# Step 0's q first on GpSimd's queue, another order of the attention steps, routing one step earlier

## The chip, the cores and the metric

One core of a Trainium2 chip runs the whole kernel. The metric is the device time of one execution in microseconds; the time before is the median of three runs.

## The reference

Attention with normalised q and k over 8 batches, 12 heads, 448 tokens and 64 columns a head, then a layer of 8 experts to which each token is routed by a hash of its id.

```python
def _attn_ref(q, k, v, g_q, g_k):          # (8, 12, 448, 64)
    q_n, k_n = rmsnorm(q, g_q), rmsnorm(k, g_k)      # x / sqrt(mean(x*x) + 1e-6) * g
    scores = scale * np.matmul(q_n, k_n.transpose(0, 1, 3, 2))
    attn = np.exp(scores - max); attn = attn / (sum + 1e-9)
    return np.matmul(attn, v)
def _moe_ref(x, token_ids, w1, w2):        # x (3584, 768), w1 (8, 768, 1024), w2 (8, 1024, 768)
    expert_idx = token_ids * 2654435761 % 8
    for e in range(8):
        out[mask] = np.maximum(x[mask] @ w1[e], 0) @ w2[e]
```

## The kernel before

The kernel has an attention stage and an expert stage. In both the order on each engine is the order of the code (`manual_schedule`).

**Attention** runs in 48 steps (`NS`), six a batch; step s holds a pair of heads. What a step needs is made by short operations that the code names with two-letter words. `sqq`, `sqk` square q and k (`prep_sq`, L359, on VectorE, or on ScalarE with the flag `@A`); `sumq`, `sumk` add the squares up by 16 matmuls with the identity (`prep_sum`, L379); `redq`, `redk` reduce them (L394, VectorE); `ln` and `er` give the reciprocal root on ScalarE (L401, L405); `nq`, `nk` multiply by it (L415, VectorE); `Tq`, `Tk` transpose on PE (L576); `qT`, `kT` copy the transposes to SBUF (L598, VectorE, or ScalarE with `@A`). `sc:s.j` is one of the four score products of step s (L620), `exp:s.j` its exponential on ScalarE (L637: 896 columns, or 448 for j = 3), `av:s.p` the product with v (L647), `rec` and `x` the division on VectorE (L679, L686). `v:c` copies a chunk of v (L436). `zero:n` clears parts of buffers (L732), `gain:n` prepares the gains of k (L188), `spin:n` issues n matmuls of 448 columns on a cleared tile, whose result nobody reads (L779).

The order is written out by hand as a text of such words: one for the first two batches, with step and group numbers, and one named `steady`, which runs once for each of the other six. `emit` (L842) turns it into instructions.

PSUM holds three double banks for scores (`ps_sc`), one bank for sums and transposes (`ps_qk`) and one for the product with v. Sums and transposes with the flag `@S` take one of the score banks instead (`turn_bank`, L374). Steps 0 and 5 stand alone; the others are prepared in pairs. Step 0's and 5's q and k transposes lie in one and the same bank.

Step 0's q and k come in fp32 through the queues of SyncE and ScalarE (`load_heads`, `load_one_q`); the other q, k and v through GpSimd's queue, pair by pair, then batch by batch, in the order of the code. A load on GpSimd's queue waits, among others, for the load eight places ahead of it. `hooks` (L792) puts loads of later batches, of weights, and the **routing** into certain steps: `SIDE` and `AV_SIDE` (L784 to L790) name for each step the routing's VectorE operations (m1 to m15) and its small matmuls (m5a, m7a, m13a, m14a), which write into the bank of that step's product with v. From the routing come row numbers (`gidx`), by which GpSimd gathers the first three tiles of expert 0's tokens; `early_xT` (L632) transposes them in score banks.

**Experts**: eight times two products, 480 or 512 token columns wide: `gemm1` (L941) with a ReLU on ScalarE or VectorE, then `gemm2` (L956) in four token tiles, copied from PSUM by ScalarE and VectorE in turn and scattered to the output by GpSimd (L975). The last tile of all (`last`) has 96 tokens and goes out in two copies, 512 columns and 256, and one scatter. Weights come through GpSimd's queue; expert 2's lie in the first buffers of q and k.

## Time and profile before

| | before |
|---|---|
| median of three timed runs | 345.65 us (344.89 to 346.58) |
| the profiled execution | 343.94 us |
| its span, first to last instruction | 342.4 us |
| PE, matmuls | 327.5 us (96%) |
| PE, weight loads | 228.6 us (67%) |
| VectorE | 201.8 us (59%) |
| ScalarE | 188.6 us (55%) |
| GpSimd | 147.7 us (43%) |

In the page's 40 slices ScalarE and VectorE read 8 or 9 tenths through the first half, the attention, and 1 to 4 in the second, the experts; PE reads 9 from the second slice to the last but one. The shares of the whole span are means over two stages with different limits, so the stages are read apart. Times in all rows are microseconds from the span's start, unless marked ns.

### The profile page before, as it was taken

Reading aid. Unit: us, or ns where it says so; the run is one execution under the profiler, and the core shown is the slowest. Engines: PE = TensorE matmul, PEld = TensorE weight load, DVE = VectorE, ACT = ScalarE, POOL = GpSimd, SP = SyncE. Lnnn points to the kernel's source line nnn. Section 1 sums busy time; section 2 is a strip of 40 time slices with the busy share of each in tenths; the row PEclk is TensorE's granted clock in tenths of the full one; section 3 lists DMA queues with packets and bytes.
Section 4 is the critical chain, followed back from the end, with each engine's and each line's share of the span. In section 5 each row is a group of like instructions: output and inputs, shape, how many; then the busy total and the mean of one; then the engine's idle time right before and its main releaser. Section 6 shows DMA issues by size and latency. Waiting matters only on the chain. (4 is left out here: it accounts for less than half of the span.)

```text
span 342.4 us, 9198 instructions
## 1 busy us (share of the span) xinstructions
PE 327.5 (96%) x3893; PEld 228.6 (67%) x3893; DVE 201.8 (59%) x433; ACT 188.6 (55%) x286; POOL 147.7 (43%) x203
## 2 busy tenths in 40 slices
PE   4999999999999999999999999999999999999992
PEld 2577777776777777666677767677676776767761
DVE  3799999998989899976693243232332323323210
ACT  3599999999999999989442212212122120220210
POOL 8799935225330100003555854538555474202122
PEclk9999999999999999999999999999999999999997
DMA  8999999999999999032579899999999999403012
GB/s 138 217 200 202 202 236 200 239 202 227 201 244 211 254 210 233 13 82 71 127 147 247 169 204 249 261 278 244 252 272 262 259 243 278 174 0 133 22 79 88
DMA packets 42498, 64.80 MB, mean 189 GB/s; under 512 B 9687, under 2 KB 30623, under 8 KB 42200
## 3 DMA queue, kind: packets, MB, share of 16 engines
q0 software_dynamic: 38688, 58.09, 84.1%
q1 hardware_dynamic: 3456, 5.90, 5.6%
q8 instruction: 31, 0.51, 0.6%
q10 hardware_dynamic: 312, 0.21, 0.2%
q14 instruction: 11, 0.09, 0.1%
HBM read 89.29 MB, written 17.30 MB: 311 GB/s over the span
## 5 line engine op out<-in xcount | busy, mean ns | idle before, releaser
L642 ACT ACTIVATE expT<-sc_ps 128x896 bf16<-128x896 f32 x144 | 125.5, 973 | 1.6 <-PE sc_ps L626 1.3
L962 PEld LDWEIGHTS <-h_sb 128*128 128x128 f16 (+1 forms) x512 | 51.2, 104 | 30.0
L962 PE MATMUL o_ps<-w_sb,h_sb 128*128 128x512 f16 (+3 forms) x384 | 66.2, 326 | 0.0
L975 POOL DMA_INDIRECT out_dram<-o_sb,gidx x32 | 33.9, 1058 | 65.2 <-ACT o_sb L972 31.3
L949 ACT ACTIVATE h_sb<-h_ps 128x480 f16<-128x480 f32 (+1 forms) x36 | 19.9, 552 | 68.1 <-PE h_ps L945 68.1
L229 POOL DMA_INDIRECT kr<-x_scratch,gidx x32 | 33.5, 1047 | 52.1 <-DVE gidx L557 37.8
L945 PEld LDWEIGHTS <-w_sb 128*128 128x128 f16 x288 | 38.9, 136 | 16.2
L945 PE MATMUL h_ps<-xT,w_sb 128*128 128x480 f16 x240 | 49.4, 366 | 0.0
L972 ACT COPY o_sb<-o_ps 128x768 f32<-128x768 f32 x16 | 12.8, 798 | 61.4 <-PE o_ps L962 61.4
L951 DVE TENSOR_SCALAR h_sb<-h_ps 128x480 f16<-128x480 f32 x28 | 18.4, 658 | 47.2 <-PE h_ps L945 47.2
L626 PE MATMUL sc_ps<-qT,kT 64*128 64x448 f16 x288 | 44.5, 356 | 1.4 <-ACT expT L642 0.7
L660 PEld LDWEIGHTS <-expT 128*128 128x128 bf16 x864 | 37.8, 97 | 10.1 <-DVE x_sb L691 4.4
L660 PE MATMUL av_ps<-v,expT 128*128 128x65 bf16 x864 | 43.3, 193 | 0.1
L972 DVE COPY o_sb<-o_ps 128x768 f32<-128x768 f32 (+1 forms) x15 | 14.3, 956 | 31.5 <-PE o_ps L962 27.2
L691 DVE TENSOR_TENSOR x_sb<-av_ps,srec 128x448 f16<-128x448 f32 x48 | 29.9, 622 | 1.4
L303 POOL DMA_DIRECT2D vr<-in_v_dram x36 | 23.8, 671 | 15.6 <-DMA kr<-in_k_dram 6.8
L645 ACT ACTIVATE expT<-sc_ps 128x448 bf16<-128x448 f32 x48 | 29.4, 613 | 0.0
L384 PEld LDWEIGHTS <-ident 128*128 128x128 f16 x576 | 23.0, 99 | 8.5 <-issue 4.8
L241 DVE COPY xT<-xT_ps 128x768 f16<-128x768 f16 x25 | 13.8, 552 | 22.6 <-PE xT_ps L240 22.4
L665 PE MATMUL av_ps<-v,expT 128*128 128x130 bf16 x144 | 25.0, 220 | 0.0
L962 PE MATMUL o_ps<-kr,h_sb 128*128 128x512 f16 (+3 forms) x128 | 22.1, 326 | 0.0
L626 PEld LDWEIGHTS <-kT 64*128 64x128 f16 x288 | 12.6, 93 | 11.4 <-issue 2.5
(211 smaller groups left out, 453.0 us busy)
## 6 DMA issues: line engine op xcount, KB each, us to landing
w_sb<-in_moe_w_dram POOLq DMA_DIRECT2D x18, 512.0 KB, 10.9
w_sb<-in_moe_w_dram POOLq DMA_DIRECT2D x8, 768.0 KB, 13.7
kr<-in_k_dram POOLq DMA_DIRECT2D x7, 672.0 KB, 14.3
qr<-in_q_dram POOLq DMA_DIRECT2D x7, 672.0 KB, 12.5
x_scratch<-x_sb SPq DMA_DIRECT2D x15, 288.0 KB, 6.1
w_sb<-in_moe_w_dram POOLq DMA_DIRECT2D x2, 1536.0 KB, 26.5
qr<-in_moe_w_dram POOLq DMA_DIRECT2D x6, 512.0 KB, 15.6
vr<-in_v_dram POOLq DMA_DIRECT2D x14, 192.0 KB, 11.7
```

Of the source, the lines that this page charges most:

```text
L229: nc.gpsimd.indirect_dma_start(out=xg[0:idx.shape[0], :], out_offset=None, in_=x_dram[0:rows, :], in_offset=bass.IndirectOffsetOnAxis(ap=i ...
L303: eng.dma_start(out=dst[64 * half:64 * half + 64, :, s0:s0 + cnt, :].rearrange("p n s d -> p n (s d)"), in_=runs(t, h0 + HP * hh, 1, n, to ...
L626: nc.tensor.matmul(sc[:, hh, :S], lhsT=kT[64 * hh:64 * hh + 64, P * j:P * j + P], rhs=qT[64 * hh:64 * hh + 64, :], start=True, stop=True)
L642: nc.scalar.activation(expT[:, 2 * j:2 * j + 2, :], sc[:, :, :S], AF.Exp, bias=0.0, scale=1.0)
L645: nc.scalar.activation(expT[:, 6, :], sc[:, 0, :S], AF.Exp, bias=0.0, scale=1.0)
L660: nc.tensor.matmul(av[:, 2 * t + hh, :], lhsT=expT[:, tl(hh, j), P * t:P * t + P], rhs=v8[:, i, vs(hh, j), 0:D + 1], start=(hh == 0 and t ...
L665: nc.tensor.matmul(av[:, 2 * t:2 * t + 2, :], lhsT=expT[:, 6, P * t:P * t + P], rhs=v8[:, i, 0::7, 0:D + 1], start=False, stop=False)
L691: nc.vector.tensor_tensor(out=xs[b][:, :, hp * D:hp * D + D], in0=av[:, :, :D], in1=srec[:, :, None].to_broadcast([P, SL, D]), op=ALU.mult)
L945: nc.tensor.matmul(h_ps[:, :c1 - c0], lhsT=w1v[:, co, fo, :], rhs=xT[:, co, c0:c1], start=(co == 0), stop=(co == CO - 1))
L962: nc.tensor.matmul(o_ps[d0 > 0][0:w, d0:d1], lhsT=h_sb[:, fo, col * P:col * P + w], rhs=w2_sb[:, fo, d0:d1], start=(fo == 0), stop=(fo == ...
L972: (nc.vector.tensor_copy if col % 2 else nc.scalar.copy)(o_sb[0:w], o_ps[0][0:w])
L975: scat = nc.gpsimd.indirect_dma_start(out=out[:, :], out_offset=bass.IndirectOffsetOnAxis(ap=idx[0:w], axis=0), in_=o_sb[0:w], in_offset=N ...
```

## The change

- Step 0's two q loads go first on GpSimd's queue, ahead of all other loads there; before, one was on SyncE's and one on ScalarE's. The loads of the gains move from ScalarE's queue to SyncE's, and that of the token ids behind the loads of step 5.
- The text of the order is another one. In the first two batches: all clears of VectorE stand in front; 17 warming matmuls, then 2, 4 and 5, stand where 6, 5, 4 and 3 were; step 0's sums and transposes use score banks; the squares of step 1's k and of step 5's k go to ScalarE, k's copies of steps 0, 5 and 8 to VectorE, q's copy of step 0 to ScalarE; steps 3 and 4, and 6 and 7, are interleaved otherwise. In the steady text some words change places.
- A step that stands alone has a bank for each of its two transposes.
- `SIDE`, `AV_SIDE` and the early gathers come one step earlier.
- The 256 columns of the last tile are copied by ScalarE instead of VectorE.
- Expert 2's second weight comes in two loads of half the size.

```diff
--- before.py
+++ after.py
@@ -124,7 +124,7 @@
 
     def setup():
         for c, src in enumerate((g_q, g_k)):
-            nc.scalar.dma_start(out=grow[:, c],
+            nc.sync.dma_start(out=grow[:, c],
                                 in_=bass.AP(tensor=src.tensor, offset=src.offset,
                                             ap=[[0, 1], [0, 2], [1, D]]))
     def setup1():
@@ -211,7 +211,9 @@
     def load_w2(e, w2_sb, dyn=None):
         src = moe_w2[e] if dyn is None else moe_w2[bass.ds(dyn, 1)].rearrange("o f d -> (o f) d")
         rows = "(fo p) d -> p fo d" if e == 0 else "(p fo) d -> p fo d"
-        nc.gpsimd.dma_start(out=w2_sb[:], in_=src.rearrange(rows, fo=FO))
+        n = FO // 2 if e == 2 else FO
+        for f in range(0, FO, n):
+            nc.gpsimd.dma_start(out=w2_sb[:, f:f + n], in_=src.rearrange(rows, fo=FO)[:, f:f + n])
         return w2_sb
 
     def new_w1(pool):
@@ -582,9 +584,7 @@
                     nc.tensor.transpose(T[:, P * o:P * o + P],
                                         n8[:, x].rearrange("p i d -> p (i d)"), ident16[:])
                 return
-            if (s, 1) not in qkt:
-                qkt[s, 1] = qkt[s, 0] = ps_qk.tile([P, 512], FP32, name="qkT_ps")[:].bitcast(FP16)
-            T = qkt[s, a]
+            T = qkt[s, a] = turn_bank(flag).bitcast(FP16)
             n8 = n8_one[:, 4 * a:4 * a + 4 + a].rearrange("p x i d -> p x (i d)")
             if not a:
                 for x in range(4):
@@ -746,6 +746,7 @@
                 nc.scalar.copy(raw(1, HP - 1)[:, 0::7], z[:, 0:2])
                 nc.scalar.copy(raw(0, HP - 1)[64:P, 3::4], z[64:P, 0:2])
                 load_one(HP - 1)
+                setup1()
             elif part == 6:
                 zero_kv(V, v_bufs[0])
             elif part == 7:
@@ -754,9 +755,8 @@
                 V.memset(v8_all[0:64, :, :, 7, D], 0.0)
 
         load_heads([nc.sync, nc.scalar, nc.sync, nc.scalar], first[:, 1:2], k, 0, 1)
-        load_one_q([nc.sync, nc.scalar], first[:, 0], 0)
+        load_one_q([nc.gpsimd] * 2, first[:, 0], 0)
         setup()
-        setup1()
         nc.vector.memset(warm, 0.0)
         load_pairs(k, k_bufs, 0, 1, 0, HP, 2)
         make_identity(nc, ident16[:])
@@ -781,13 +781,13 @@
                 nc.tensor.matmul(wps[:, 0:448], lhsT=warm[:, 0:P], rhs=warm[:, 0:448],
                                  start=True, stop=True)
 
-        AV_SIDE = {NS - 11: (m5a, m5b), NS - 10: (m7a, m7b), NS - 5: (m14a, m14b)}
+        AV_SIDE = {NS - 12: (m5a, m5b), NS - 11: (m7a, m7b), NS - 6: (m14a, m14b)}
         for i in range(2):
-            AV_SIDE[NS - 7 + i] = (lambda av, i=i: m13a(av, i), lambda av, i=i: m13b(av, i))
+            AV_SIDE[NS - 8 + i] = (lambda av, i=i: m13a(av, i), lambda av, i=i: m13b(av, i))
         half = lambda f, *es: [lambda e=e: f(e) for e in es]
-        SIDE = {NS - 12: (m1, m2, m3), NS - 11: (m4,), NS - 9: [m8, m9] + half(m10, 0, 1),
-                NS - 8: half(m11, 0, 1) + half(m12, 0), NS - 7: half(m12, 1), NS - 6: (n2,),
-                NS - 4: (m15,), NS - 3: (n3,)}
+        SIDE = {NS - 13: (m1, m2, m3), NS - 12: (m4,), NS - 10: [m8, m9] + half(m10, 0, 1),
+                NS - 9: half(m11, 0, 1) + half(m12, 0), NS - 8: half(m12, 1), NS - 7: (n2,),
+                NS - 5: (m15,), NS - 4: (n3,)}
 
         def hooks(s):
             if s >= NS:
@@ -801,8 +801,8 @@
                 load(4, "kv")
             if hp == 3 and 1 <= b and b + 4 < B:
                 load(b + 4, "qkv")
-            if NS - 4 <= s < NS - 5 + KT:
-                c = s - NS + 4
+            if NS - 5 <= s < NS - 6 + KT:
+                c = s - NS + 5
                 gather(xg_e[:, c], gidx[:, c:c + 1], N_EARLY)
             if s == 24:
                 w_tiles[0] = [load_w1(0, new_w1(w_pool))]
@@ -858,46 +858,46 @@
         emit("""
-            zero:0 zero:2 zero:7 zero:3 spin:6 sqk:0.0 sqq@A:0.0 sumk:0.0 zero:6 redk:0.0
-            sqk:1.0 sumq:0.0 ln:0.1.2 spin:5 sumk@S:1.0 zero:1 er:0.1.2 nk:0 redq:0.0
...
+            zero:0 zero:1 zero:2 zero:6 zero:7 spin:17 sqk:0.0 zero:3 sqq@A:0.0 sumk@S:0.0
+            redk:0.0 sumq@S:0.0 ln:0.1.2 redq:0.0 er:0.1.2 ln:0.0.1 er:0.0.1 sqk@A:1.0
...
         steady = """
-            sc:0.3 exp:0.1 exp:0.3 av:-1.0 av:-1.1 av:-1.2 nq:2 sc:1.0 kT:2 rec:-1 x:-1
-            exp:1.0 Tq:2 qT:2 sc:1.1 sc:1.2 av:0.0 sc:1.3 av:0.1 sumk:1.0 exp:1.1 nk:4
...
+            exp:0.3 av:-1.0 av:-1.1 nq:2 av:-1.2 kT:2 sc:1.0 exp:1.0 rec:-1 x:-1 Tq:2 sc:1.1
+            sc:1.2 exp:1.1 qT:2 av:0.0 sqq:2.0 sc:1.3 exp:1.2 sumk:1.0 nk:4 av:0.1 exp:1.3
...
@@ -971,7 +971,7 @@
                 o_sb = m_o.tile([P, DIN], FP32, name="o_sb")
                 (nc.vector.tensor_copy if col % 2 else nc.scalar.copy)(o_sb[0:w], o_ps[0][0:w])
             else:
-                nc.vector.tensor_copy(o_sb[0:w, 512:DIN], o_ps[1][0:w, 512:DIN])
+                nc.scalar.copy(o_sb[0:w, 512:DIN], o_ps[1][0:w, 512:DIN])
             scat = nc.gpsimd.indirect_dma_start(
                 out=out[:, :], out_offset=bass.IndirectOffsetOnAxis(ap=idx[0:w], axis=0),
                 in_=o_sb[0:w], in_offset=None, bounds_check=N - 1, oob_is_err=False)
```

On GpSimd, from its first load on (`expT` is the buffer that step 0's q and k share, `kr` and `qr` are those of k and q, `vr` of v, `ident` the identity). Before:

```order
L314 DMA kr_68<-in_k_dram 128x2x448
masks.py:197 MEMSET ident_75 128x128
masks.py:199 ISA
masks.py:199 AFFINE_SELECT ident_75<-ident_75 128x128
L314 DMA qr_67<-in_q_dram 128x2x448
```

After:

```order
L298 DMA expT<-in_q_dram 64x2x256
L299 DMA expT<-in_q_dram 64x2x192
L316 DMA kr_68<-in_k_dram 128x2x448
masks.py:197 MEMSET ident_75 128x128
masks.py:199 ISA
masks.py:199 AFFINE_SELECT ident_75<-ident_75 128x128
L316 DMA qr_67<-in_q_dram 128x2x448
```

Step 0's q has come in front of all else on this queue, two loads of it.

On ScalarE, from the square of step 0's q to the first exponentials (`ss` the sums of squares, `rr` the reciprocal roots, `expT` from 128x896 on the exponentials). Before:

```order
L370 ACTIVATE sq_q<-expT 128x8x16x4
L403 ACTIVATE ss<-ss,eps_col 128x8
L409 ACTIVATE rr<-ss 128x16
L403 ACTIVATE ss<-ss,eps_col 128x8
L409 ACTIVATE rr<-ss 128x16
L612 ACTIVATE kT<-qkT_ps,g_col 128x512
L403 ACTIVATE ss<-ss,eps_col 128x2x14
L409 ACTIVATE rr<-ss 128x2x28
L642 ACTIVATE expT<-sc_ps 128x896
L645 ACTIVATE expT<-sc_ps 128x448
L642 ACTIVATE expT<-sc_ps 128x896 x2
L370 ACTIVATE sq_q<-qr_67 128x8x16x4
```

After:

```order
L372 ACTIVATE sq_q<-expT 128x8x16x4
L405 ACTIVATE ss<-ss,eps_col 128x8
L411 ACTIVATE rr<-ss 128x16
L405 ACTIVATE ss<-ss,eps_col 128x8
L411 ACTIVATE rr<-ss 128x16
L372 ACTIVATE sq_k<-kr_68 128x14x16x4
L612 ACTIVATE qT<-sc_ps 128x448
L405 ACTIVATE ss<-ss,eps_col 128x2x14
L411 ACTIVATE rr<-ss 128x2x28
L642 ACTIVATE expT<-sc_ps 128x896 x2
L372 ACTIVATE sq_k<-kr_68 128x8x16x4
L645 ACTIVATE expT<-sc_ps 128x448
```

A square of k has come in ahead of the first copy, which is now q's, and another square of k behind the second exponential.

On ScalarE, around the copies of steps 6 and 8. Before:

```order
L612 ACTIVATE qT<-sc_ps 128x896
L642 ACTIVATE expT<-sc_ps 128x896 x2
L403 ACTIVATE ss<-ss,eps_col 128x2x28
L409 ACTIVATE rr<-ss 128x2x56
L642 ACTIVATE expT<-sc_ps 128x896 x3
L645 ACTIVATE expT<-sc_ps 128x448
L642 ACTIVATE expT<-sc_ps 128x896
L612 ACTIVATE kT<-sc_ps,g_col 128x1024
L645 ACTIVATE expT<-sc_ps 128x448
```

After:

```order
L612 ACTIVATE qT<-sc_ps 128x896
L405 ACTIVATE ss<-ss,eps_col 128x2x28
L411 ACTIVATE rr<-ss 128x2x56
L642 ACTIVATE expT<-sc_ps 128x896 x3
L645 ACTIVATE expT<-sc_ps 128x448 x2
L642 ACTIVATE expT<-sc_ps 128x896 x6
L645 ACTIVATE expT<-sc_ps 128x448
```

The copy of k of 1024 columns is gone from here; the one of 512, some exponentials ahead of the first of these rows, is gone in the same way. Both stand on VectorE now.

## Rows read from the trace of the kernel before

**Rows 1.** Windows: stretch, length, busy time (instructions) by engine, clock, DMA share, GB/s

```profile
core 0: us, PE busy (x) PEld busy (x) DVE busy (x) ACT busy (x) POOL busy (x), PEclk, DMA share, GB/s
15.00:20.00 5.00, 5.00 (x76) 3.25 (x76) 4.72 (x11) 4.81 (x10) 4.54 (x6) 1.00 1.27 206
...
200.00:240.00 40.00, 40.00 (x252) 27.66 (x251) 12.49 (x20) 7.11 (x12) 20.59 (x25) 1.00 1.07 253
```

**Rows 2.** Windows of ScalarE alone, first exponential to last

```profile
145.00:150.00 5.00, 4.12 (x6) 1.00 0.30 59
...
sum 147.51, ACT 145.71; mean ACT 8.57
```

**Rows 3.** Timeline to the first exponential: start, duration, operation [idle before <-releaser]

```profile
1.41 2.42 PE L781 MATMUL av_ps<-hi 128*128 128x448 f16 x6 [1.41 <-DVE hi L760]
...
6.04 0.69 DVE L372 TENSOR_TENSOR sq_k<-expT 128x512 f16<-128x512 f32 x1 [3.22 <-DMA expT<-in_k_dram]
...
6.78 0.59 PE L384 MATMUL qkT_ps<-sq_k,ident 128*128 128x32 f16 x16 [2.95 <-DVE sq_k L372]
...
6.86 0.38 DVE L729 MEMSET vr<- 64x384 uint32 x1
...
7.09 0.63 ACT L370 ACTIVATE sq_q<-expT 128x512 f16<-128x512 f32 x1 [1.48 <-DMA expT<-in_q_dram]
...
8.28 2.03 PE L781 MATMUL av_ps<-hi 128*128 128x448 f16 x5
...
9.23 0.30 ACT L403 ACTIVATE ss<-ss,eps_col 128x8 f32<-128x8 f32 x1 [0.86 <-DVE one L191]
...
12.38 0.92 PE L781 MATMUL av_ps<-hi 128*128 128x448 f16 x4
...
14.14 0.92 ACT L642 ACTIVATE expT<-sc_ps 128x896 bf16<-128x896 f32 x1 [0.39 <-PE sc_ps L626]
```

**Rows 4.** Timeline of GpSimd: the issue of its first two loads

```profile
1.51 0.91 POOL L314 DMA_DIRECT2D kr<-in_k_dram  x1 [0.84 <-POOLq L1243]
...
2.96 0.78 POOL L314 DMA_DIRECT2D qr<-in_q_dram  x1
```

**Rows 5.** DMA issues at 1.51 and 16.66: count, KB each, us to landing

```profile
kr<-in_k_dram POOLq DMA_DIRECT2D x1, 224.0 KB, 4.7
...
kr<-in_k_dram POOLq DMA_DIRECT2D x1, 672.0 KB, 14.2
```

**Rows 6.** ScalarE's groups by form: count, busy us, mean ns, idle before

```profile
L612 ACT ACTIVATE kT<-qkT_ps,g_col 128x512 f16<-128x512 f16 x2 | 1.4, 687 | 3.2 <-PE qkT_ps L591 3.2
...
L612 ACT ACTIVATE kT<-sc_ps,g_col 128x1024 f16<-128x1024 f16 x1 | 1.1, 1147 | 0.0
...
L370 ACT ACTIVATE sq_q<-qr 128x512 f16<-128x512 f32 x1 | 0.6, 632 | 0.0
```

**Rows 7.** Timeline: batch 2's k, its load's issue and its squares

```profile
16.66 0.85 POOL L314 DMA_DIRECT2D kr<-in_k_dram  x1
...
32.67 0.86 DVE L372 TENSOR_TENSOR sq_k<-kr 128x1344 f16<-128x1344 f16 x1
```

**Rows 8.** Timeline at the attention's end: last exponential, third early transposes

```profile
161.03 0.62 ACT L645 ACTIVATE expT<-sc_ps 128x448 bf16<-128x448 f32 x1
...
161.84 0.34 PEld L240 LDWEIGHTS <-kr 128*128 128x128 f16 x6 [0.15 <-DMA kr<-x_scratch,gidx]
```

**Rows 9.** Timeline of the last two tiles: copies and scatters

```profile
332.98 0.80 ACT L972 COPY o_sb<-o_ps 128x768 f32<-128x768 f32 x1 [4.40 <-PE o_ps L962]
334.05 0.98 POOL L975 DMA_INDIRECT out_dram<-o_sb,gidx  x1 [1.41 <-ACT o_sb L972]
334.75 0.58 ACT L969 COPY o_sb<-o_ps 96x512 f32<-96x512 f32 x1 [0.97 <-PE o_ps L962]
335.63 0.42 DVE L974 COPY o_sb<-o_ps 96x256 f32<-96x256 f32 x1 [4.24 <-PEq L1213]
336.85 0.92 POOL L975 DMA_INDIRECT out_dram<-o_sb,gidx  x1 [1.82 <-POOLq L1213]
```

68 lines of the change are left out of this document (34 added, 34 removed).

## The prediction

> **What bounds the kernel now.** The sum is made against the profiled execution: 343.94 us, of which the span is 342.4; the median of the timed runs is 345.65. A saving is taken from both alike, and the forecast is stated on the median. I read the windows by stage first, then ScalarE's windows alone, and last the timeline at both ends.
>
> PE seems to settle it, and does not: the ends of matmuls are modelled. In the expert stage PE is the bound, 40.00 of 40 us from 200 to 240 with DVE at 12.49 and ACT at 7.11 [rows 1]. In the attention stage PE reads 5.00 of 5 us too, but its weight loads fill only 3.25 of them, while ACT is at 4.81 and DVE at 4.72 [rows 1]. Which of the three is the bound there is seen in ScalarE alone: from the first exponential at 14.14 to the last one's end at 161.65 it is busy 145.71 of 147.51 us [rows 2]. 1.80 us of idle time are all that a better order could take out of it, and 0.88 of them lie in 145 to 150 [rows 2], where PE does the routing's small matmuls. So the end is: start of the first exponential, plus ScalarE's work, plus its idle time, plus the hand-over to the experts, plus some 172 us of PE, plus the last tile's way out. Each part of the change is priced in that sum.
>
> **The change part by part.**
>
> *The first exponential: 1.85 us earlier.* Before, step 0's k is squared at 6.04 after a wait for its DMA, its sums start on PE at 6.78, q's squares at 7.09 after q's DMA, q's logarithm only at 9.23, the exponential at 14.14 [rows 3]. Three things lie between. q's reduce stands behind k's normalising on VectorE, and both sums share one bank. Five warming matmuls of 2.03 us stand at 8.28 in front of step 1's sums and step 0's transposes [rows 3]. And both transposes of step 0 use one bank, so that k's copy on ScalarE and q's on VectorE come one after the other. The new order gives these sums and transposes banks of their own and puts both reduces ahead of the normalising.
>
> q's loads: the first load on GpSimd's queue was issued at 1.51 [rows 4] and landed 4.7 later, at 6.2 [rows 5]. q's two now stand in its place, the second some 0.8 behind the first (a load there takes 0.78 or 0.91 to issue, [rows 4]); so q is there between 6.2 and 7.0, about as before (7.09). What the move frees is issue time on ScalarE's and SyncE's queues.
>
> PE: 17 warming matmuls now run from 1.41. Six took 2.42 us and five 2.03, so 0.39 for each more; four later ones took 0.92 [rows 3]. For 448 columns that is TensorE's 1.2 GHz first and its 2.4 GHz later. All 17 at the first pace end at 8.1; with the last third at the second, at 7.0. I take 7.0: between 6.78 and 12.38 [rows 3] the clock had risen, with pauses between, and these 17 have none.
>
> From there: sums (0.59, [rows 3]) and reduces to 8.2; two pairs of logarithm (0.30, [rows 3]) and exponential on ScalarE to 9.1; the square of step 1's k, which moves to ScalarE, 1.0 by its copies (0.69 for 512 columns, 1.15 for 1024, [rows 6]), to 10.1; PE's sum of it and q's transposes, half a microsecond each, to 11.0; q's copy on ScalarE (under 0.69) to 11.65; the score to 12.05; step 1's logarithm pair, ahead of the first exponential in both orders, to 12.3. That is 1.85 under 14.14. Bounds: 0.7 if all warming matmuls run at the slow pace; 2.7 if k lands 0.8 sooner, since the loads of steps 1 and 2 now start behind q.
>
> *ScalarE's work behind it: 1.2 us less.* Step 5's copy of k (0.69) and step 8's (1.15) go to VectorE, and one square of 512 columns (0.63) comes to ScalarE [rows 6]: 0.69 + 1.15 - 0.63 = 1.2, on the path one to one. The cover is VectorE, at 4.72 of 5 us here [rows 1]. It gets two copies, 1.8 us at ScalarE's durations and less at its own, and gives away that square (0.6) and one of 896 columns; its two clears of v (0.38 each, [rows 3]) move in front of k's arrival, where it idles 3.22 us [rows 3]. So it ends with no more work behind 6 us than it had. If that cover were gone, the 1.2 would be.
>
> *The steady order*: nothing. The exponentials keep their order, the 1.80 us of idle time stay. Bounds: 0.6 less to 0.6 more.
>
> *Routing one step earlier*: the same matmuls and VectorE operations stand beside other scores, so the 0.88 us of idle time move and stay; bounds 0.9 less to 0.9 more. The first gathers come sooner, so PE's transposes of the third no longer start at 161.84 after 0.15 of waiting for one [rows 8]. But they need the bank that the last exponential (161.03, 0.62 long) frees at 161.65 [rows 8]: that is late next, and only 0.15 is gained.
>
> *The last tile: 0.3 us.* VectorE's copy of 256 columns started at 335.63, took 0.42, and the scatter began at 336.85, 0.80 after its end; a tile copied by one engine went out 0.27 after its copy (332.98 + 0.80, scatter at 334.05) [rows 9]. ScalarE's 0.80 for 768 columns and 0.58 for 512 [rows 9] give 0.36 for 256. If it is the wait for a second engine that cost the rest, the move saves 0.06 + 0.53 = 0.6; if not, 0.06. No row tells which, so I take the middle.
>
> *w2 of the second expert in two loads, token ids and gains on other queues*: nothing. GpSimd's one issue more hides under its waits for copied tiles, and the experts' PE has no wait for a weight in 200 to 240 [rows 1]; without that cover it would cost that one issue, 0.8.
>
> Sum: 1.85 + 1.2 + 0.15 + 0.3 = **3.5 us**: 340.4 profiled, **342.1** on the median.
>
> **The rivals.**
>
> *The loads set the ramp.* From 15 to 20 the DMA engines move 206 GB/s [rows 1] and no load lands sooner because steps run sooner. The tightest rows: batch 2's k was issued at 16.66 [rows 7] and landed 14.2 later [rows 5], at 30.9; VectorE squares it at 32.67 [rows 7]. That is 1.8 us of slack, and the new order asks for it 1.9 sooner (1.85 + 0.69 - 0.63), which costs 0.1 and is hidden by the exponentials already scored. If q's two issues in front push all later loads back by their 1.5 us, 0.3 of the slack is left, and of the gains 0.3, step 8's 1.15 and 0.45 at the end: 345.65 - 1.9 = 343.75. For it: every load of GpSimd's queue now stands behind q. Against: the bytes ahead of batch 2's k are the same.
>
> *VectorE's clears keep GpSimd from writing q's loads.* All clears now run in the microseconds in which GpSimd writes them. In the trace GpSimd's first load, beside clears, took 0.91 us and its next 0.78 [rows 4]: 0.13 at most. If q waited for the last clear instead, some 2.4 us (an estimate: the two of 0.38 and shorter ones), it would land at 8.6 or later; the start would lose 0.45 instead of gaining 1.85, and the other 1.65 leave 345.65 - 1.2 = 344.45. The Trainium skill speaks here against the change: "SBUF — State Buffer", section "Who interferes with whom", has some VectorE operations hold a pair of ports that GpSimd needs, and the later one blocked entirely. By that rule, the 344.45; by the row, nothing. "DMA: Bandwidth & Descriptors", section "Latency and other measured facts", adds a first byte after about 1 us from GpSimd's queue against 0.6 us from the others: q 0.4 later, an estimate from that page, and the start as much; the trace, in which a load issued first lands after 4.7 us, shows the transfers ahead to matter more.
>
> *Slower: a hole in the steady order.* That text is run six times. It puts a square of the batch after next ahead of a normalising of k on VectorE, and the next step's first score behind three attention parts on PE. If each run opens a hole of the size of the one in 145 to 150 (0.88, [rows 2]), 6 x 0.88 = 5.3 less the 3.5 gives 347.5; it decides from 3.5 / 6 = 0.58 us a run. For it: ScalarE has no slack, so every late score is paid. Against: the two orders differ there by a few swaps.
>
> **How the numbers follow.** The forecast, 342.1, has 0.60; its own range is 340.5 to 343.7 (first exponential 0.7 to 2.7, last tile 0.06 to 0.6, idle time half a microsecond either way). The loads have 0.23, the clears 0.08, the hole 0.09. The range 340.5 to 344.9 takes in the forecast, the loads and the clears, and leaves out the hole and the ends of the others. 0.5%, 1.73 us, is about what a measurement of this kernel can tell from no change: faster is under 343.9, slower over 347.4. Faster: nearly all of the forecast and half of the loads' case, 0.70. Slower: most of the hole's, 0.08. Same: 0.22.
>
> **What would show it.** The first exponential at 11.5 to 13.4; PE's first sums at 7 rather than 8; no square on VectorE waiting for a DMA around 30; ScalarE busy some 144.5 us between first and last exponential, with under 2.5 idle; the last scatter 0.3 behind ScalarE's copy. The forecast is wrong if ScalarE shows new waits for scores in 50 to 140, if q's squares start past 8, or if VectorE waits for batch 2's k.

## The result, and the profile after

The changed kernel takes 341.98 us (341.21 to 342.21, four runs) against 346.12 (344.89 to 346.59, four runs) for the kernel before: a ratio of 0.9888, 95% interval 0.9866 to 0.9910, so 4.1 us less. The forecast was 342.1, with 340.5 to 344.9 as its range. Measured again beside other runs of before, the ratio is 0.9891 (0.9866 to 0.9916), 3.7 us less.

The two profiled executions differ by only 2.1 us, 342.4 and 340.3 of span, half of what the medians differ by. That was the first thing to explain. In this table the first column gives when the first exponential starts, each further one how long the stretch from there to its heading lasts, in the first traces and in all later ones; together they are the span.

| trace | first exponential | from there to the last one's end | to the first expert matmul | to the last scatter | to the end | span |
|---|---|---|---|---|---|---|
| before | 14.14 | 147.51 | 1.61 | 173.59 | 5.53 | 342.4 |
| before, again | 15.81 | 148.09 | 1.45 | 173.33 | 5.53 | 344.2 |
| changed | 11.81 | 148.43 | 1.45 | 172.70 | 5.95 | 340.3 |
| changed, again | 12.27 | 147.83 | 1.45 | 172.75 | 5.95 | 340.3 |
| a_route | 12.21 | 147.53 | 1.45 | 172.69 | 5.86 | 339.7 |
| a_first | 15.06 | 147.56 | 1.46 | 172.74 | 6.11 | 342.9 |
| b_spin17 | 13.20 | 148.73 | 1.46 | 173.32 | 5.79 | 342.5 |
| a_spin6 | 12.35 | 147.70 | 1.45 | 172.85 | 5.96 | 340.3 |
| a_q | 12.06 | 148.89 | 1.45 | 172.70 | 5.95 | 341.0 |
| a_kT | 12.38 | 153.38 | 1.45 | 172.73 | 5.87 | 345.8 |
| b_kTV | 15.66 | 150.11 | 1.45 | 173.33 | 5.57 | 346.1 |
| a_tail | 12.08 | 148.83 | 1.45 | 173.89 | 5.91 | 342.2 |
| a_best1 | 10.96 | 150.25 | 2.63 | 173.28 | 5.85 | 343.0 |
| a_route_w2 | 12.11 | 149.89 | 2.56 | 173.27 | 5.99 | 343.8 |

The start of the changed kernel, from the timeline (start, duration, operation, idle time before it and its releaser), which answers to [rows 3] and [rows 4]:

```profile
1.52 0.80 POOL L298 DMA_DIRECT2D expT<-in_q_dram  x1 [0.86 <-POOLq L1243]
2.31 0.68 POOL L299 DMA_DIRECT2D expT<-in_q_dram  x1
...
1.42 5.74 PE L781 MATMUL av_ps<-hi 128*128 128x448 f16 x17 [1.42 <-DVE hi L760]
...
5.20 0.69 DVE L374 TENSOR_TENSOR sq_k<-expT 128x512 f16<-128x512 f32 x1 [1.30 <-DMA expT<-in_k_dram]
...
5.49 0.63 ACT L372 ACTIVATE sq_q<-expT 128x512 f16<-128x512 f32 x1 [2.46 <-DMA expT<-in_q_dram]
...
7.00 0.56 PE L386 MATMUL sc_ps<-sq_k,ident 128*128 128x32 f16 x16
...
7.80 1.30 PE L781 MATMUL av_ps<-hi 128*128 128x448 f16 x6
...
10.65 0.54 ACT L612 ACTIVATE qT<-sc_ps 128x448 f16<-128x448 f16 x1 [1.00 <-PE sc_ps L591]
...
11.81 1.71 ACT L642 ACTIVATE expT<-sc_ps 128x896 bf16<-128x896 f32 x2
```

q is there at 5.49 instead of 7.09, k at 5.20 instead of 6.04. The sums wait for neither, but for the 17 warming matmuls, behind which they start at 7.00, as forecast. The six warming matmuls behind the sums take 1.30, or 0.22 each; before, five took 2.03, or 0.41 each.

ScalarE's windows in the changed kernel (length, busy time and count, clock, DMA share, GB/s), which answer to [rows 2]; the first is the stretch from the first exponential to the last one's end, the others are parts of it:

```profile
11.81:160.24 148.43, 145.49 (x214) 1.00 1.10 194
20.00:50.00 30.00, 29.43 (x45) 1.00 1.33 212
50.00:130.00 80.00, 79.97 (x117) 1.00 1.24 221
130.00:160.24 30.24, 28.36 (x41) 1.00 0.43 103
```

Here the forecast fails: it had ScalarE's work down by 1.2 and its idle time unchanged. Idle time went from 1.80 to 2.94 us, and busy time fell by 0.22 only (in the second traces below, idle time from 2.19 to 2.52, busy time by 0.58). Busy time hides some lateness too: three exponentials in a row are recorded as 2.54 us, two of 0.81 and a last one of 0.92, so each record reaches 0.11 into the next, and a score up to 0.11 late leaves no gap. I therefore also added up, over all of ScalarE's instructions between the first and the last exponential, the distance to the next start beyond the shortest such distance of the same form. These late starts, as they are called below, are 5.03 and 5.42 us in the two traces of before, 6.93 and 6.17 in those of the changed kernel.

The end of the changed kernel, from the timeline, which answers to [rows 9]:

```profile
332.22 0.98 POOL L975 DMA_INDIRECT out_dram<-o_sb,gidx  x1 [1.41 <-ACT o_sb L972]
332.92 0.58 ACT L969 COPY o_sb<-o_ps 96x512 f32<-96x512 f32 x1 [0.97 <-PE o_ps L962]
333.75 0.37 ACT L974 COPY o_sb<-o_ps 96x256 f32<-96x256 f32 x1 [0.25 <-PE o_ps L962]
334.39 0.92 POOL L975 DMA_INDIRECT out_dram<-o_sb,gidx  x1 [1.19 <-POOLq L1213]
```

The last scatter starts 1.47 behind the start of the first copy instead of 2.10, and 0.27 behind the end of the last copy instead of 0.80. But the program ends 5.95 behind it instead of 5.53.

### The profile page after: what moved, and what is told of

The parts are those of the page before. It is cut to its first block, busy times and chain, and to the rows that moved or that the text cites. A ratio compares the mean times of both kernels' runs of the same rounds, so it can differ in the third digit from the quotient of the medians.

```text
span 340.3 us, 9213 instructions
## 1 busy us (share of the span) xinstructions
PE 328.1 (96%) x3903; PEld 228.7 (67%) x3903; DVE 200.7 (59%) x432; ACT 189.4 (56%) x287; POOL 148.8 (44%) x206
## 5 line engine op out<-in xcount | busy, mean ns | idle before, releaser
L231 POOL DMA_INDIRECT kr<-x_scratch,gidx x32 | 32.6, 1020 | 53.0 <-DVE oc L568 37.8
L945 PE MATMUL h_ps<-xT,qr 128*128 128x480 f16 x96 | 19.8, 366 | 0.0
```

What stands on the lines that cost most here:

```text
L231: nc.gpsimd.indirect_dma_start(out=xg[0:idx.shape[0], :], out_offset=None, in_=x_dram[0:rows, :], in_offset=bass.IndirectOffsetOnAxis(ap=i ...
L945: nc.tensor.matmul(h_ps[:, :c1 - c0], lhsT=w1v[:, co, fo, :], rhs=xT[:, co, c0:c1], start=(co == 0), stop=(co == CO - 1))
```

## The experiments

The kernels ran on four chips, each beside runs of before on its chip, and are compared by their ratio to these; microseconds follow from that ratio and those runs (345.1 to 346.1). The names of kernels made from before begin with b, of those made from the changed kernel with a.

| kernel | edit | median us | before on the same chip | ratio, 95% interval |
|---|---|---|---|---|
| before_again | none | 345.24 | 345.10 | 1.0003 (0.9983 to 1.0023) |
| after_again | none | 341.40 | 345.10 | 0.9891 (0.9866 to 0.9916) |
| a_route | routing as before | 340.98 | 345.10 | 0.9882 (0.9852 to 0.9913) |
| a_first | first two batches as before | 344.64 | 345.10 | 0.9987 (0.9968 to 1.0006) |
| b_spin17 | 17 warming matmuls | 345.04 | 345.85 | 0.9969 (0.9942 to 0.9996) |
| a_spin6 | 6 warming matmuls | 342.93 | 345.85 | 0.9921 (0.9893 to 0.9950) |
| a_q | q's queues as before | 343.25 | 345.85 | 0.9925 (0.9895 to 0.9954) |
| a_kT | two copies back on ScalarE | 346.29 | 345.85 | 0.9999 (0.9973 to 1.0025) |
| b_kTV | two copies on VectorE | 346.21 | 346.04 | 1.0016 (0.9999 to 1.0032) |
| a_tail | last tile as before | 343.93 | 346.04 | 0.9951 (0.9930 to 0.9972) |
| a_best1 | start in another order, routing as before | 344.27 | 346.04 | 0.9948 (0.9927 to 0.9970) |
| a_route_w2 | routing and w2 as before | 344.23 | 346.06 | 0.9935 (0.9911 to 0.9959) |

The first four rows are of one chip, the next four of a second, then three of a third and one of a fourth. On the last three chips the changed kernel itself did not run, and there all its variants lie at 0.992 or above, also a_route_w2, which differs from a_route (0.9882) by one load of a weight alone. So a difference between such a variant and the changed kernel's 0.989 can hold something of the chip, which no run tells apart from the edit; differences between kernels on one chip cannot.

The runs' mean granted clocks say more. All 123 runs of before (before_again among them), b_spin17 and b_kTV have 0.993 or more, and so have those of the changed kernel, a_route, a_first and a_spin6; 0.992 or less stands in 29 of the 45 runs of a_q, a_kT, a_tail, a_best1 and a_route_w2. In the traces such a mean goes with stretches at half clock (1.2 GHz) in mid-kernel: two in a_kT, one each in a_q, a_best1 and a_route_w2, none in the other ten. In a_best1 the six runs with it take 344.1 to 344.7 us, the two without 343.1 and 343.3; in a_tail the three with it are the slowest, 345.4 to 345.6.

**Both kernels once more.** No edit.

> The kernel before, unchanged. The first pair of profiles differs by 2.1 us of span (342.4 and 340.3), the medians by 4.1 (346.12 and 341.98). Theory 'the first profile of before was a fast execution': a second one is 1 to 2 us longer, and its trace names the place, as waits of ScalarE for scores between 14 and 162 us (1.8 us of idle time in the first profile, 3 or more here). Rival 'the traces are typical and the difference lies outside the span': the span is again 342.4 within 0.4, first exponential at 14.1, end of the last at 161.6, and the time is 3 us or more above the span.

> The changed kernel, unchanged. Both theories: 342.0 within 0.4, ratio to before 0.988 to 0.990; first exponential 11.8, end of the last 160.2, last scatter 0.3 behind the last copy. If the changed kernel varies as much as before does (2.7 us from fastest to slowest), the range of its times widens past 1.0 us.

The start of before in its second trace, from the timeline (PE and ScalarE) and ScalarE's window from its first exponential to its last:

```profile
8.51 2.03 PE L781 MATMUL av_ps<-hi 128*128 128x448 f16 x5
...
13.58 1.70 PE L781 MATMUL av_ps<-hi 128*128 128x448 f16 x4
...
13.82 0.69 ACT L612 ACTIVATE kT<-qkT_ps,g_col 128x512 f16<-128x512 f16 x1 [3.83 <-PE qkT_ps L591]
...
15.81 0.92 ACT L642 ACTIVATE expT<-sc_ps 128x896 bf16<-128x896 f32 x1 [0.81 <-PE sc_ps L626]
...
15.81:163.90 148.09, 145.90 (x214) 1.00 1.08 189
```

The first profile of before was indeed shorter than most executions: its 343.94 lies below all but three of the 35 timed runs of before on this chip. The place is another than expected: not waits for scores in the attention (2.19 us of idle time, 0.4 more than in the first trace), but the start. The four warming matmuls behind step 0's transposes took 0.92 in [rows 3] and take 1.70 here. That is 0.23 and 0.42 each: TensorE was at its 2.4 GHz there in the first trace, and is still at 1.2 GHz here. The five in front of the transposes stand 0.23 later than in [rows 3], the four behind them 1.20, the first exponential 1.67: what lies between runs at the slow pace. Of the 1.8 us between the two spans, this is nearly all. In the changed kernel the matmuls behind the first sums are fast in both traces (1.30 for six). Its times spread over 1.0 and 1.3 us in four and six runs, those of before over 2.5 and 3.2 in 23 and 12.

The changed kernel's second trace shows something else, on VectorE:

```profile
10.22 0.63 DVE L374 TENSOR_TENSOR sq_q<-qr 128x896 f16<-128x896 f16 x1 [1.20 <-DMA qr<-in_q_dram]
```

Its sums start 0.75 sooner than in the first trace (6.25 for 7.00), its first exponential 0.46 later (12.27 for 11.81). Between them VectorE waits 1.20 us for step 1's q, whose logarithm stands ahead of the first exponential on ScalarE. That q's load is issued at 4.26 in the changed kernel, behind step 0's q, and lands 5.9 later; before, it is issued at 2.96 [rows 4] and lands 5.6 later, and VectorE squares it at 9.32 without a wait. So in this execution a load sets the first exponential, and sums that end sooner bring nothing. (a_tail waits 0.61 at the same place, a_route_w2 0.26, the first trace not at all.)

**The first two batches as before.** The first text, q's queues, the gains, the token ids and the shared bank.

```diff
-            T = qkt[s, a] = turn_bank(flag).bitcast(FP16)
+            if (s, 1) not in qkt:
+                qkt[s, 1] = qkt[s, 0] = ps_qk.tile([P, 512], FP32, name="qkT_ps")[:].bitcast(FP16)
+            T = qkt[s, a]
...
-        load_one_q([nc.gpsimd] * 2, first[:, 0], 0)
+        load_one_q([nc.sync, nc.scalar], first[:, 0], 0)
...
-            zero:0 zero:1 zero:2 zero:6 zero:7 spin:17 sqk:0.0 zero:3 sqq@A:0.0 sumk@S:0.0
...
+            zero:0 zero:2 zero:7 zero:3 spin:6 sqk:0.0 sqq@A:0.0 sumk:0.0 zero:6 redk:0.0
```

> The changed kernel with the first two batches as before: the order's first text, the queues of q's loads, of the gains and the token ids, the shared bank of step 0's transposes. Theory 'of the new first text only its start counts': the first exponential is at 14.1 again (2.3 later), ScalarE gets its copies back (1.06 by start-to-start distances) and loses 1.2 us of late starts, so 342.0 + 2.3 + 1.06 - 1.2 = 344.2. Rival 'ScalarE's work counts one to one, the late starts are chance': 342.0 + 2.3 + 1.06 = 345.4. If the gain of the change lies elsewhere: under 343.

It lies 0.1% under before and 1.0% over the changed kernel: 3.3 us of the whole gain are in this part. The steady order, the routing, the last tile and w2, which it still has, are together worth 0.13%, which its interval doesn't tell from nothing. ScalarE's window in its trace:

```profile
15.06:162.62 147.56, 145.73 (x214) 1.00 1.08 191
```

From the first exponential to the last one's end it needs 147.56, with the old distribution of work, as long as before and no longer than the changed kernel (147.83 and 148.43). So the 1.06 us of work that ScalarE is spared in the new text (0.585 + 0.996 less one square of 0.52, by the distances between starts) don't show in the stage's length. The first exponential came at 15.06, not at the 14.1 of the first trace, so that both expected times rested on the wrong start; of the two theories the first, that only the start of the new text counts, is the one that the stages bear out.

**The warming matmuls alone**, in each kernel.

```diff
-            zero:0 zero:2 zero:7 zero:3 spin:6 sqk:0.0 sqq@A:0.0 sumk:0.0 zero:6 redk:0.0
+            zero:0 zero:2 zero:7 zero:3 spin:17 sqk:0.0 sqq@A:0.0 sumk:0.0 zero:6 redk:0.0
```

> The kernel before with 17 warming matmuls in place of its first 6, nothing else. Theory 'the pace of TensorE at the start': in the traces of before it falls from 0.37 to 0.19 us for 448 columns only after the first sums, once at 10.9, once past 13.6; with 17 in a row it falls before the sums, so the five warming matmuls behind them take 1.0 instead of 2.03, the first exponential stands at 12.6 to 13.2 (14.14 and 15.81 before), the time is 345.1 - 2.1 = 343.0 and its range under 1.5 us (before: 2.5). Rival 'the banks, the order and the queue of q make the start': first exponential at 14 or later, since the sums start later than 6.8; 345.1 within 0.5, range as before.

```diff
-            zero:0 zero:1 zero:2 zero:6 zero:7 spin:17 sqk:0.0 zero:3 sqq@A:0.0 sumk@S:0.0
+            zero:0 zero:1 zero:2 zero:6 zero:7 spin:6 sqk:0.0 zero:3 sqq@A:0.0 sumk@S:0.0
```

> The changed kernel with 6 warming matmuls in front instead of 17. Theory 'the pace at the start': matmuls of 448 columns still take 0.37 behind the first sums, the first exponential moves from 11.8 to 12.3 to 12.8 to 14, the time rises by 1 to 2 to some 343 and varies by over 1.5 us. Rival 'the 17 only hold up the sums': sums at 5.9 instead of 6.3 to 7.0, first exponential at 11.5 or sooner, time 341.4 or less.

Timelines, first of before with 17, with its first exponential and ScalarE's window:

```profile
1.42 5.07 PE L781 MATMUL av_ps<-hi 128*128 128x448 f16 x17 [1.42 <-DVE hi L760]
...
8.46 1.11 PE L781 MATMUL av_ps<-hi 128*128 128x448 f16 x5
...
13.20 0.92 ACT L642 ACTIVATE expT<-sc_ps 128x896 bf16<-128x896 f32 x1 [0.40 <-PE sc_ps L626]
...
13.20:161.93 148.73, 145.93 (x214) 1.00 1.08 192
```

then of the changed kernel with 6:

```profile
1.42 2.42 PE L781 MATMUL av_ps<-hi 128*128 128x448 f16 x6 [1.42 <-DVE hi L760]
...
6.84 2.40 PE L781 MATMUL av_ps<-hi 128*128 128x448 f16 x6
...
12.27 1.12 PE L781 MATMUL av_ps<-hi 128*128 128x448 f16 x5
```

The pace theory holds for the mechanism. With 17 in a row the five behind the sums take 1.11 instead of 2.03; with 6 the later six take 2.40 instead of 1.30. The first exponential of b_spin17 stands at 13.20 as expected. The price was put too high: before gains 0.3% by it, 1.1 us and not 2.1, and its range is 2.2, not under 1.5. The trace doesn't settle why. It took 344.06, 1.0 under the kernel's own median, and its longer attention (148.73 with 2.80 of idle time against 147.51 and 148.09) holds two scores that come 0.52 and 0.40 late at 155.74 and 158.96, a thing that comes and goes in both orders (last section). The changed kernel loses 1.1 (0.9921 against 0.9890), but across chips and with overlapping intervals, so that this is not shown. Its trace, with the first exponential at 12.35, is that of the shortest of its ten runs and doesn't show what the others lost. Warming up is worth about 1 us of the 3.3, by b_spin17. Evenness is not shown to come from it: a_spin6's times spread over 3.0 us, but those of a_q and a_tail, with all 17, over 3.8 and 2.9.

**q's queue.**

```diff
-        load_one_q([nc.gpsimd] * 2, first[:, 0], 0)
+        load_one_q([nc.sync, nc.scalar], first[:, 0], 0)
```

> The changed kernel with step 0's q loads on the queues of SyncE and ScalarE, as before. Theory 'q first on GpSimd's queue is part of the start': k lands at 6.0 again (5.1 to 5.5 in the changed kernel), q at 7.1 (5.5), the sums' squares end at 7.7 instead of 6.2, so first exponential 0.6 to 1.2 later and time 342.0 to 342.6. Rival 'the 17 warming matmuls hide it, and step 1's q, which lands 1 to 1.5 us sooner, pays it back': first exponential within 0.3 of 12.0, time 341.4 within 0.3.

The time says the first theory (1.2 us over the changed kernel by the ratios, across chips), the trace the rival: k is squared at 6.32 and q at 6.96, the sums stand at 7.06 and 7.64, right behind the 17 warming matmuls, and the first exponential at 12.06. Its longer attention comes from elsewhere, a stretch at the slower clock in 155 to 160 (below). Beside a_spin6, on the same chip, it is 0.3 us slower, which the intervals don't tell from nothing. So what q's queue is worth isn't settled; nothing in the trace shows a loss by it.

**The two copies of k, moved alone**, back to ScalarE in the changed kernel and to VectorE in before.

```diff
-            exp:3.1 Tk@S:5 sc:3.3 kT:5 x:2 sumq:3.0 exp:3.2 sc:4.3 sc:4.2 exp:3.3 redq:3.0
+            exp:3.1 Tk@S:5 sc:3.3 kT@A:5 x:2 sumq:3.0 exp:3.2 sc:4.3 sc:4.2 exp:3.3 redq:3.0
...
-            sumq:5.0 x:5 exp:6.2 av:6.0 sc:7.2 exp:7.1 exp:7.2 kT:8 sc:8.0 sqq:5.1 redq:5.0
+            sumq:5.0 x:5 exp:6.2 av:6.0 sc:7.2 exp:7.1 exp:7.2 kT@A:8 sc:8.0 sqq:5.1 redq:5.0
```

> The changed kernel with the copies of k of steps 5 and 8 on ScalarE again. Theory 'ScalarE's work counts one to one': 0.585 + 0.996 (distances between starts in the trace of before) more, time 341.4 + 1.6 = 343.0, late starts of ScalarE in 20 to 50 us as in the changed kernel (1.2 to 1.5). Rival 'what ScalarE saves there it loses to waits for a full VectorE': the late starts in 20 to 50 fall by about a microsecond, time 341.4 to 342.0.

```diff
-            exp:3.2 sumk@S:4.0 nq:5 x:2 Tq:5 sc:4.3 av:3.0 redq:3.0 kT@A:5 sc:4.2 sqq:4.0
+            exp:3.2 sumk@S:4.0 nq:5 x:2 Tq:5 sc:4.3 av:3.0 redq:3.0 kT:5 sc:4.2 sqq:4.0
...
-            sc:7.3 sumq:5.0 sc:7.2 sqk:5.1 av:6.0 redq:5.0 kT@A:8 exp:7.3 sqq:5.1 nk:10
+            sc:7.3 sumq:5.0 sc:7.2 sqk:5.1 av:6.0 redq:5.0 kT:8 exp:7.3 sqq:5.1 nk:10
```

> The kernel before with the copies of k of steps 5 and 8 on VectorE, nothing else. Theory 'ScalarE's work counts one to one': 0.585 + 0.996 less, so 1.6 less than the kernel before (ratio 0.9955). Rival 'VectorE is as full as ScalarE in the first batches, what leaves one comes back as a wait for the other': within 0.5 of the kernel before, late starts of ScalarE between 20 and 50 us larger by 1 or more than the 0.5 to 1.1 of the traces of before.

In before with both copies on VectorE, ScalarE's window of 20 to 50 and, from the timeline, the two copies and ScalarE's longest waits behind them:

```profile
20.00:50.00 30.00, 27.28 (x42) 1.00 1.33 212
...
31.06 0.48 DVE L615 TENSOR_SCALAR kT<-qkT_ps,g_col 128x512 f16<-128x512 f16 x1 [0.42 <-PE qkT_ps L591]
...
34.08 0.92 ACT L642 ACTIVATE expT<-sc_ps 128x896 bf16<-128x896 f32 x1 [0.53 <-PE sc_ps L626]
...
43.10 0.74 DVE L615 TENSOR_SCALAR kT<-sc_ps,g_col 128x1024 f16<-128x1024 f16 x1
...
44.31 3.35 ACT L642 ACTIVATE expT<-sc_ps 128x896 bf16<-128x896 f32 x4 [0.65 <-PE sc_ps L626]
```

In before the copies bring nothing on VectorE: 1.0016, where 1.58 us less work on ScalarE would be 0.9955. ScalarE now idles 2.72 us in 20 to 50, where the two traces of before have 0.40 and 0.69, and its late starts there are 3.6 instead of 0.6 and 1.1. Not all of that is the copies': this trace is of the longest of its ten runs, and 1.16 of it is a wait for a reduce at 21.78, ahead of the first moved copy. What lies behind the copies can be counted by exponentials, of which every kernel has 192. From the 13th to the 51st, the stretch with both copies, this trace needs 31.94 us, the four traces with before's order and the copies on ScalarE 31.50 to 31.59. The work saved, 1.58, is gone there, and 0.4 more; the late starts from 31 to 50 are 2.06, against 0.03 and 0.01. The rival holds: in this order, what leaves ScalarE comes back as waits for scores.

The other way the loss is larger than either theory had: 3.8 us by the ratios, and 3.0 and 3.4 beside a_q and a_spin6 on the same chip. In the changed kernel with the copies on ScalarE, the windows of 40 to 50 and a row each of PE and ScalarE from the timeline:

```profile
40.00:45.00 5.00, 3.30 (x4) 0.66 1.19 267
45.00:50.00 5.00, 4.43 (x7) 1.00 1.33 204
...
41.63 0.93 PE L626 MATMUL sc_ps<-qT,kT 64*128 64x448 f16 x4 [2.02 <-ACT kT L612]
...
45.31 0.54 ACT L645 ACTIVATE expT<-sc_ps 128x448 bf16<-128x448 f32 x1 [1.30 <-PE sc_ps L629]
```

PE waits 2.02 us for the copy that stands behind exponentials on ScalarE, the granted clock falls from 1.00 to a mean of 0.66 over these 5 us (at 0.5 it is 1.2 GHz), and the scores come late a second time. From the 13th exponential to the 51st this trace needs 34.96 us, seven traces of the changed order with the copies on VectorE 30.5 to 30.8: a loss of over 4 us in the very stretch, of which 1.58 are the copies' work. This trace is of the longest of ten runs, so that the medians hold less of it. In the changed order, then, the two copies belong on VectorE, by more than either theory had; in before's they gain nothing there.

**The routing and the early gathers at the steps of before**, alone and with w2 in one load.

```diff
-            if NS - 5 <= s < NS - 6 + KT:
-                c = s - NS + 5
+            if NS - 4 <= s < NS - 5 + KT:
+                c = s - NS + 4
```

(All keys of `SIDE` and `AV_SIDE` go one up in the same way; in a_route_w2 also `n = FO`.)

> The changed kernel with the routing's operations and the early gathers at the steps of before. Theory 'the earlier routing costs waits': between 130 us and the last exponential ScalarE's starts are late by 2.0 us as before instead of 2.8, the first matmuls of the experts start 0.85 - 0.15 = 0.7 sooner than 161.70, time 341.3. Rival 'the waits move with the routing and stay': within 0.3 of 342.0; the hand-over from the last exponential's end to the first expert matmul is 1.6 again instead of 1.46.

> The changed kernel with the routing and the early gathers at the steps of before, and the second expert's second weight in one load, as before. Two questions. First: in all traces of the changed kernel and its variants the last scatter lands 3.6 to 3.7 us behind its start, in those of before 3.2 to 3.4. Theory 'the additional load moves the last scatter to another place among GpSimd's loads': 3.2 here, the end 5.5 behind its start, 0.4 gained, ratio 0.987. Rival 'something else in the change': 3.7, ratio 0.988. Second: four variants of the changed kernel that ran on two other chips lie at 0.992 to 0.995 of before, the changed kernel on two chips at 0.989. If that is the chips and not the variants, this one lies at 0.992 or above on one of those; if it is the variants, at 0.989 or under on any.

ScalarE's last window in a_route:

```profile
130.00:159.74 29.74, 28.70 (x42) 1.00 0.45 108
```

Alone, 0.9882 against 0.9891: no difference. Its late starts from 130 on are 1.7, those of the changed kernel 2.8 and 1.95, of before 1.98 and 1.95; what the first trace of the changed kernel has more there is one score that comes 0.91 late at 157, which is absent from its second trace and not this edit's (last section). The hand-over is 1.45, with the old gathers and the new.

a_route_w2 answers its first question with the rival: 5.99 us from the last scatter to the end with w2 in one load. Its second is answered in part: 0.9935 is not the 0.989 or under that stood for the variants, but it came on a chip of which neither branch had a run, so that a chip's share and the one load of w2 aren't told apart. Its trace is also of the longest of eight runs.

**The last tile.**

```diff
-                nc.scalar.copy(o_sb[0:w, 512:DIN], o_ps[1][0:w, 512:DIN])
+                nc.vector.tensor_copy(o_sb[0:w, 512:DIN], o_ps[1][0:w, 512:DIN])
```

> The changed kernel with VectorE copying the last tile's 256 columns, as before. Theory 'the last scatter's start is gained, its way out gives most back': the last scatter starts 0.6 later behind the end of the first copy (2.10 instead of 1.47 behind its start), and ends 5.5 behind its start instead of 5.95, so 0.2 in all: ratio 0.989 as the changed kernel, within the spread. Rival 'the earlier scatter counts in full': 0.6 slower, the time behind the scatter's start 5.9 again.

Its last rows, from the timeline:

```profile
334.15 0.58 ACT L969 COPY o_sb<-o_ps 96x512 f32<-96x512 f32 x1 [0.97 <-PE o_ps L962]
335.04 0.42 DVE L974 COPY o_sb<-o_ps 96x256 f32<-96x256 f32 x1 [4.24 <-PEq L1213]
336.25 0.92 POOL L975 DMA_INDIRECT out_dram<-o_sb,gidx  x1 [1.82 <-POOLq L1213]
```

The scatter again starts 2.10 behind the first copy's start and 0.79 behind the second's end, so the 0.6 is shown to be this edit's. The way out stays at 5.91, so that in the trace the rival holds: the copy on ScalarE counts in full, and what makes the way out 0.4 longer isn't this copy. The median is 2.1 us over the changed kernel's ratio, across chips. The tail explains 0.6 of it; the trace shows another 0.5 in the experts' stage before the tail, three of the ten runs have the lower mean clock, and the rest I can't place.

**Another order at the start**, meant to beat both kernels: step 0's transposes, copies and first score ahead of step 1's sums, the first exponential ahead of step 1's logarithm, and the routing as before.

```diff
-            gain:0 spin:2 nk:0 spin:4 gain:1 Tk@S:0 nq:0 sumk@S:1.0 gain:2 sqq:1.0 Tq@S:0
-            redk:1.0 sumq:1.0 kT:0 redq:1.0 qT@A:0 sc:0.0 ln:1 er:1 sc:0.1 spin:5 exp:0.0
-            nk:1 Tk@S:1 sc:0.3 nq:1 Tq:1 sqk:2.0.0 kT:1 qT:1 exp:0.1 sqq:2.0.0 v:0
-            sqk@A:2.0.1 sc:0.2 exp:0.3 sumk@S:2.0 sc:1.0 sqq@A:2.0.1 exp:0.2 exp:1.0
+            gain:0 spin:2 nk:0 spin:4 gain:1 Tk@S:0 nq:0 gain:2 Tq@S:0 kT:0 sumk@S:1.0
+            redk:1.0 qT@A:0 sqq:1.0 sc:0.0 sumq:1.0 redq:1.0 exp:0.0 sc:0.1 ln:1 er:1 spin:5
+            nk:1 Tk@S:1 sc:0.3 nq:1 Tq:1 kT:1 sqk:2.0.0 qT:1 exp:0.1 sqq:2.0.0 v:0
+            sqk@A:2.0.1 sc:0.2 exp:0.3 sc:1.0 sumk@S:2.0 sqq@A:2.0.1 exp:0.2 exp:1.0
```

> The changed kernel with the routing at the steps of before, and at the start step 0's transposes, copies and first score ahead of step 1's sums on TensorE and VectorE, the first exponential ahead of step 1's logarithm, k's copy of step 1 ahead of the next squares. Theory 'step 0 waits for step 1's q at the start': the first exponential at 11.2 whether step 1's q lands at 9 or at 10.2 (11.8 to 12.4 in the changed kernel), exponentials of step 1 from 15.5 (16.0 to 16.9), so 0.5 less at the start and 0.4 less from the routing: ratio 0.9865. Rival 'the loads set the ramp': what the start gains is waited for between 15 and 50 us, ratio 0.988 to 0.989.

Its timeline at the start and at the attention's end, and the window of 160 to 165:

```profile
10.96 0.92 ACT L642 ACTIVATE expT<-sc_ps 128x896 bf16<-128x896 f32 x1 [0.45 <-PE sc_ps L626]
...
17.94 0.33 ACT L405 ACTIVATE ss<-ss,eps_col 128x44 f32<-128x44 f32 x1 [0.72 <-DVE ss L401]
...
158.97 0.63 PE L660 MATMUL av_ps<-v,expT 128*128 128x65 bf16 x12 [1.66 <-DVE x_sb L691]
...
160.00:165.00 5.00, 2.01 (x3) 0.73 0.00 0
```

The first exponential comes at 10.96, sooner than in any other trace, and the gain is gone 7 us later: step 2's logarithm stands at 17.94, behind a wait of 0.72 for VectorE's reduce, where the changed kernel has it at 17.14 and 18.04 in its two traces. In this order a still earlier first exponential is worth nothing. The rival's sentence on the ramp is borne out, though what is waited for there is VectorE's and PE's work on step 2, not a load; its ratio isn't, for 0.9948 lies above the changed kernel's, though across chips. Its trace shows a pause of PE of 1.66 that ends at 158.97, a slower clock behind it, and a hand-over of 2.63 instead of 1.45; a_route_w2 shows the same three (a pause of 1.67, a hand-over of 2.56), a_route, with the same routing on the first chip, none of them. That isn't a chance of the two traces: the lower mean clock stands in six of a_best1's eight runs and in seven of a_route_w2's, in none of a_route's four. No version ran that beats the changed kernel beyond the intervals.

## Why the prediction was right, and where it was not

The total is right (341.98 for 342.1) and so was the direction; the saving, forecast at 3.5, was 4.1 and 3.7 us. That it came so near is luck in part: two large steps missed in opposite ways and nearly cancelled, and the median of before moved from 345.65 to 346.12. (The terms of the forecast's own range add up to 344.0 at the upper end, not 343.7; the stated range takes in both.)

- **What bounds the kernel**: held. In every trace the span is the start of the first exponential, ScalarE's stretch, the hand-over, the experts and the way out, and the difference of any two traces is the sum of theirs.
- **The first exponential**: forecast at 12.3, 11.5 to 13.4; it stands at 11.81 and 12.27, and PE's sums at 7.00 and, in the second trace, 6.25. The chain that was worked out is the one seen in the first trace; in the second the load of step 1's q sets the time, which the chain did not hold. What failed is the size of the gain, 1.85, and with it the sentence that a saving is taken alike from the profiled execution and from the median. The 14.14 was an early start: the old first text has 14.14, 15.06, 15.66 and 15.81 in four traces, mean 15.2; the changed kernel and the variants that leave its start alone (a_route, a_tail, a_route_w2) have 11.8 to 12.3, mean 12.1. So the term is 3.1. By b_spin17 about 1 us of it is the warming; the banks, the order and q's queue weren't tried one by one with a clear outcome. A sign of the early start was at hand: the profile's 343.94 lay under every timed run of before.
- **ScalarE's work, 1.2 less and "on the path one to one"**: failed. b_kTV gains nothing by the same two copies, a_first is no slower in its stretch with them, and the late starts between 10 and 50 grow from 1.0 and 1.5 us to 2.2 and 2.3. Counted by exponentials, the changed kernel gains 0.8 and 1.1 us from the 13th to the 51st, where the two copies stood (30.81 and 30.49 for 31.57 and 31.59), and gives back 0.8 and 0.7 ahead of the 13th (10.70 and 11.15 for 9.88 and 10.44), where the squares have come in and where the new start waits for loads and for VectorE. The named cover, VectorE at 4.72 of 5 us, was too thin: counting its operations showed no more work for it, but not that what waits behind them comes later.
- **The steady order and the routing**: nothing each, as forecast. From 50 to 130 ScalarE idles 0.03 us (before 0.17), so the hole, the slower rival, is not there. The waits for scores beside the routing moved and stayed: 0.78 and 0.46 late at 146.78 and 150.07 before, 0.67 and 0.74 at 141.08 and 145.08 after.
- **The hand-over, 0.15**: failed, for the reason given for the median. The wait of 0.15 for the third gather [rows 8] was that execution's; the second trace of before has 1.45 as well.
- **The last tile**: forecast 0.3 between 0.06 and 0.6; the scatter starts 0.63 sooner, the upper end (it is the wait for a second engine, as a_tail shows). But the end comes later behind the scatter in all ten traces of the changed kernel and its variants (5.85 to 6.11, against 5.53 to 5.79 in the four of before and its variants). Undoing the copy (a_tail), or the routing and w2's second load (a_route_w2), doesn't take that away, so its cause is open; 5.79 and 5.85 lie close enough that chance isn't excluded.
- **w2, the token ids and the gains**: nothing seen, as forecast.
- **The rival of the clears**: not there. GpSimd issued q's two loads in 0.80 and 0.68 beside VectorE's clears and the loads of k and q behind them in 0.77 and 0.74, where these took 0.91 and 0.78 before, and step 0's q came 1.6 sooner. The prediction put the 344.45 down to a rule of the Trainium skill, "SBUF — State Buffer", section "Who interferes with whom". That was a misreading: the section doesn't count a memset among the operations that take the shared ports on this chip, and the trace agrees with it. What a later first byte, from the Trainium skill's "DMA: Bandwidth & Descriptors", section "Latency and other measured facts", cost is not seen apart; it did not outweigh the earlier place in the queue.
- **The rival of the loads**: not at the place named, but nearer the start. VectorE squares batch 2's k without a wait (31.36 and 32.26); it does wait for step 2's k, 0.43 and 0.89 us before 13.53 and 14.44, and in the second trace 1.20 for step 1's q before 10.22, ahead of the first exponential. As for the ramp itself, a_best1 shows that an even earlier first exponential is waited for within 7 us.

By the second pair of traces the sum is 3.54 at the first exponential, 0.26 in ScalarE's stretch, nothing at the hand-over, 0.58 up to the last scatter, less 0.42 behind it: 3.96, for spans of 344.2 and 340.3. The forecast had 1.85, 1.2, 0.15 and 0.3.

## What to carry to other kernels

Compare the profiled execution's time with the timed runs before taking a stage's start from it: where it lies under all of them, some stage in it was lucky, and a second trace of the same kernel says which. Where two engines are both over nine tenths full, moving work from one to the other is worth nothing until an experiment shows it; moving it back, in another order, may cost more than the work. Give TensorE something to do without a pause until its first real matmuls: that was worth about 1 us here. Run the changed kernel beside each of its variants on the same chip, and look at the granted clock of every run, before calling a difference of 1 or 2 us an edit's.
